# A first transform stage with 128-row matmuls over a block-diagonal table, and a new order of all operations

## The chip, the cores and the metric

The kernel runs on one core of a Trainium2 chip. A core has TensorE (PE, matmuls into PSUM), VectorE (DVE), ScalarE (ACT), GpSimd (POOL), and SyncE (SP), whose queue issues most of the DMAs here; ACT's queue issues a few. Each engine works through its own instructions in the order in which they stand, and semaphores make one engine wait for another. The metric is the device time of one launch in microseconds (us). Three runs of the kernel before took 208.42, 209.37 and 209.37 us; the median is 209.37 us.

## The reference

Two independent halves read inputs of sequence length 2048 and width 640, and their outputs are laid side by side (2048 x 1280, bf16).

```python
# half A: a diagonal complex state-space layer
Lam_bar = jnp.exp(dt * Lam); B_bar = ((Lam_bar - 1.0) / Lam)[:, None] * Bmat
Bu = jnp.einsum("bld,pd->blp", x + 0j, B_bar)
for t in range(L):
    h = Lam_bar[None, :] * h + Bu[:, t, :]
y = 2.0 * jnp.einsum("blp,dp->bld", hseq, Cmat).real + x * Dskip[None, None, :]
# half B: a four-tap convolution of k, times v, a long convolution with ssm_k by FFT, times q
kv = k_shift * v
y_f = rfft(pad(kv)) * rfft(pad(ssm_k))
y = irfft(y_f)[:, :S, :] + kv * ssm_D
return q * y
```

## The kernel before

One SBUF tensor, `arena`, holds everything; `acc` is the whole of PSUM, eight banks. Names such as `s1h0_4` below are those that the program gives its operations: kind, then half or group.

Half A splits the 2048 steps into 128 blocks of 16. Matmuls at L554 and L575 build the input of every level of a 16-step scan (`up2`, `up1`, `up0`; results leave PSUM by ACT or DVE at L571, L595, L620). Then a scan over the 128 blocks runs in two halves of five groups (`coarse`): for each half a matmul that swaps real and imaginary parts (`cs_v`, L646 and L647), a rotation on DVE, the scan itself (L654), a second swap (`cs_k`) and the rotation back, which ends at L660 (`cs_h`). `down` spreads the block states over the 16 steps again (PE at L677 and L679, added back at L695 or L697), and `project` forms the output: 20 matmuls at L714 for each of the sixteen rows of 128 steps (`C0` to `C15`), an addition at L716 and a store at L720. Its factor x times Dskip is an own instruction at L706 (`xd`), on DVE or POOL, and needs rows of x that L705 loads (`ld_r`).

Half B is a transform of length 4096 in two stages, for two halves of 320 channels, first for the filter (`h`) and then for the signal (`k`). Stage 1 (`s1`, L832) handles eight columns per operation. A column holds four channels on four blocks of 32 partitions. The table `F1` has two channel columns (`me` marks the parity of the partition's block of 32), so one matmul covers two channels, 64 partitions: a column takes 2 (halves of the output) x 2 (pairs of channels) matmuls of a 64x64 tile on 64 moving columns, 32 for one operation. The two channel pairs use different row halves of the array and write different PSUM banks. The result, 128x1024, is copied out by ACT or DVE at L837 (`e1`). Stage 2 is L850 with its copies at L863 (`s2`, `e2`), the product of the two spectra is on DVE and POOL at L874 to L881, the way back is L895 with L900 (`r2`) and L916 with L928 (`r1`), and L940 stores.

The signal of half B comes from a chain through one buffer: k is loaded transposed (L769), multiplied by four taps and summed (L197 or L198, L795), multiplied by v (L796), written to DRAM as rows (L802, `pl`) and read back in another layout (L812, `rl`). The second half of the filter (`ld_h1`, L762, four loads) goes into a buffer that `coarse` uses until `cs_h1`; then one small load (`ld_D`, L750) and one small addition (`addD1`, L764) must be done before the first of the ten operations `s1h1` may start.

What runs where and when is a table of numbers written out by hand or by a planner, `ORDER`: `"123A0"` says that operation 123 is issued next, on engine A (A is ACT, V DVE, G POOL, T PE, S SP), with PSUM bank 0. All engines' queues follow from it. `emit` adds the semaphores that the footprints in memory ask for, and an operation that writes PSUM waits until its banks have been copied out.

Of the kernel before, what the change touches and what calls it, by code (L numbers as in the profile page):

```python
# [182 lines left out]
for _name, _n in (("A", 10 * 16 * 130), ("BT", 6400), ("RR", 5120), ("W", 4096), ("G", 8192), ("XT", 10240), ("AS", 10240),  # L183
                  ("Y", 10240), ("T", 6656), ("KT", 2064), ("VT", 6144), ("H0", 5120), ("KV", 5120), ("YS", 2560), ("I3", 192),
                  ("E", 64), ("JS", 128), ("F1", 128), ("IDF", 192), ("DR", 640), ("SK", 20), ("DM", 160),
                  ("PV", 60), ("SMALL", 1400)):
    LAY.part(_name, _n)
# [31 lines left out]
def setup(c):  # L219
# [34 lines left out]
    me, mk = f(2), f(2)  # L254
# [10 lines left out]
    for b, off in ((0, 6144.0), (1, 8192.0)):  # L265
# [5 lines left out]
    P.add("f1", {V: .32}, lambda e: e.tensor_tensor(  # L271
        out=F1.rearrange("p (k s) -> p k s", s=2), in0=bc(s1.rearrange("p (k o) -> p k o", o=1), [128, 64, 2]),
        in1=bc(me.rearrange("p (o s) -> p o s", o=1), [128, 64, 2]), op=ALU.mult), outs=[F1], ins=[s1, me])
# [62 lines left out]
def params(c):  # L336
# [7 lines left out]
    for k, src in enumerate((lam_re, lam_im, ldt_in)):  # L344
        rows = pr[10 * k:10 * k + 10, :]
        P.add("ld_par", {PSP: .1}, lambda e, rows=rows, src=src: e.dma_start(
# [376 lines left out]
class PartB:  # L723
# [91 lines left out]
    def s1(self, what, hf, u):  # L815
# [11 lines left out]
        def mm(e, B):  # L827
            for i in range(8):
                for b in range(2):
                    for l in range(2):  # L830
                        ps = slice(64 * l, 64 * l + 64)
                        e.matmul(B[64 * b:64 * b + 64, 512 * l + 64 * i:512 * l + 64 * i + 64], lhsT=lh[i][ps], rhs=F[ps, b, :], start=True,  # L832
                                 stop=True, tile_position=(64 * l, 64 * b))
        P.add(f"s1{what}{hf}_{u}", {PPE: .27}, mm, ins=lh + [c.F1], group=g, nmm=32)
# [3 lines left out]
            out=out, in_=B.rearrange("p (l n k s) -> p k s l n", n=8, l=2, s=2)), outs=[out], group=g)  # L838
# [192 lines left out]
def plain_order(P):  # L1031
# [125 lines left out]
```

## Time and profile before

| what | value |
|---|---|
| median of three runs | 209.37 us (208.42 to 209.37) |
| span of the profiled execution, first to last instruction | 205.6 us |
| the median less that span | 3.8 us |
| PE busy | 180.7 us, 88% |
| DVE busy | 166.2 us, 81% |
| ACT busy | 142.5 us, 69% |
| POOL busy | 76.4 us, 37% |
| stage 1, L832: matmuls, busy | 1280, 18.2 us |
| copies of stage 1, L837: on ACT, on DVE | 34 and 6 |

A time of its own is not given for the profiled execution, only its span; what lies around the span is taken as the 3.8 us of the table. A profile line of a group reads: source line, engine, operation, what it writes and reads, how often; then busy us and the mean ns of one; then the idle time of the engine just before it and what ended it. A line of the timeline reads: start in us, length in us, engine, line, operation, shapes, count, and in brackets the idle time before it. Consecutive instructions of one line are merged in one row, and its length reaches to the end of the last, which overlaps the start of the next row.

### The profile page before, as it was taken

The page shows a single profiled execution, that of the slowest core. Times are in us where ns is not written, and L with a number is a line of the kernel's source. Part 1 is how long each engine was busy: PE and PEld are TensorE (multiplying, and loading weights), DVE is VectorE, ACT ScalarE, POOL GpSimd, SP SyncE. Part 2 cuts the span into 40 slices and gives each one's busy share as a digit, 9 for nine tenths or more (in the row PEclk, how much of TensorE's full clock was granted, in tenths as well). Part 3 has the DMA queues.
Part 4 walks back from the last instruction along what each step waited for, and adds up shares of the span by engine and source line. Part 5 has one row for each costly group of instructions (what it writes and reads, how often), then busy time and mean ns, then how long its engine had stood idle before and what let it go on. Part 6 is the DMA issues. An engine that isn't in the chain of part 4 may idle for free.

```text
span 205.6 us, 8247 instructions
## 1 busy us (share of the span) xinstructions
PE 180.7 (88%) x3713; PEld 118.7 (58%) x3713; DVE 166.2 (81%) x228; ACT 142.5 (69%) x164; POOL 76.4 (37%) x63
## 2 busy tenths in 40 slices
PE   2399999999999989768759999999999998999891
PEld 0245444554556647447546757546577776887670
DVE  4929349798949698798697989999999899988821
ACT  2628897887994889999738799996999950550000
POOL 8799900000040727037310180684910507120120
PEclk9999999999999999999965899999999999999998
DMA  4999979989999989659948990140962794166866
GB/s 124 160 195 168 183 163 168 136 187 156 228 222 180 267 135 199 109 100 129 134 141 171 161 101 3 40 129 3 212 80 67 171 218 96 66 160 168 227 165 156
DMA packets 107549, 30.20 MB, mean 147 GB/s; under 512 B 102394, under 2 KB 106874, under 8 KB 107514
## 3 DMA queue, kind: packets, MB, share of 16 engines
q1 hardware_dynamic: 107226, 29.35, 77.4%
q8 instruction: 29, 0.48, 1.1%
q10 hardware_dynamic: 288, 0.33, 0.5%
q14 instruction: 6, 0.05, 0.1%
HBM read 10.99 MB, written 7.86 MB: 92 GB/s over the span
## 4 chain that ended last, share of the span: by engine, by line
PE 46%; ACT 24%; DVE 10%; DMA 10%; issue 5%; POOL 1%; SPq 0%; DVEq 0%; ACTq 0%
PE acc L714 14%; PE acc L554 12%; ACT arena L863 8%; ACT arena L837 7%; DMA arena<-in_B_k_dram 6%; PE acc L850 5%; PE acc L679 3%; PE acc L832 3%; PE acc L895 3%; DVE arena L716 2%; PE acc L575 2%; DVE arena L874 2%; ACT arena L198 2%; DVE arena L877 2%; PE acc L916 2%
## 5 line engine op out<-in xcount | busy, mean ns | idle before, releaser
L554 PE MATMUL acc<-arena 128*64 128x512 bf16 x400 | 50.0, 403 | 3.9 <-issue 3.6
L714 PE MATMUL acc<-arena 128*128 128x320 bf16 x320 | 46.0, 300 | 1.4 <-DVE arena L716 0.8
L554 PEld LDWEIGHTS <-arena 128*64 128x64 bf16 x400 | 23.4, 112 | 26.5 <-issue 6.5
L714 PEld LDWEIGHTS <-arena 128*128 128x128 bf16 x320 | 30.4, 98 | 14.4 <-issue 0.9
L837 ACT CAST arena<-acc 128x1024 bf16<-128x1024 f32 x34 | 32.7, 1033 | 5.8 <-PE acc L832 5.6
L863 ACT CAST arena<-acc 128x960 bf16<-128x960 f32 (+1 forms) x37 | 32.5, 907 | 5.7 <-PE acc L850 4.9
L850 PE MATMUL acc<-arena 128*64 128x160 bf16 x512 | 23.2, 238 | 2.5 <-ACT arena L863 1.3
L832 PE MATMUL acc<-arena 64*64 64x64 bf16 x1280 | 18.2, 205 | 6.9 <-ACT arena L837 3.0
L706 POOL TENSOR_TENSOR arena<-arena 128x640 bf16<-128x640 bf16 x9 | 13.4, 1499 | 28.0 <-DMA arena<-in_A_x_dram 28.0
L850 PEld LDWEIGHTS <-arena 128*64 128x64 bf16 x512 | 18.2, 111 | 8.8 <-ACT arena L863 3.7
L900 ACT CAST arena<-acc 128x1024 bf16<-128x1024 f32 x16 | 15.5, 1021 | 10.8 <-PE acc L895 10.8
L832 PEld LDWEIGHTS <-arena 64*64 64x64 bf16 x1280 | 14.5, 117 | 14.0 <-ACT arena L837 6.2
L795 DVE TENSOR_TENSOR arena<-arena 128x2048 bf16<-128x2048 bf16 x14 | 17.8, 1268 | 5.8 <-ACT arena L198 5.5
L198 ACT ACTIVATE arena<-arena 128x2048 bf16<-128x2048 bf16 (+3 forms) x15 | 18.6, 1243 | 5.4 <-DMA arena<-in_B_k_dram 4.2
L697 DVE TENSOR_TENSOR arena<-acc,arena 128x1024 bf16<-128x1024 f32 (+2 forms) x17 | 19.2, 1148 | 1.4 <-ACT arena L863 0.7
L881 POOL TENSOR_TENSOR arena<-arena 128x1280 bf16<-128x1280 bf16 x3 | 8.5, 2821 | 27.5 <-DVE arena L877 27.5
L716 DVE TENSOR_TENSOR arena<-acc,arena 128x640 bf16<-128x640 f32 x16 | 13.3, 832 | 4.9 <-PE acc L714 4.8
L434 POOL TENSOR_TENSOR arena<-arena 128x1280 bf16<-128x1280 bf16 x1 | 2.3, 2331 | 32.1 <-ACT arena L198 32.1
L679 PE MATMUL acc<-arena 128*128 128x512 bf16 (+2 forms) x50 | 13.0, 346 | 0.6 <-ACT arena L837 0.5
L197 DVE TENSOR_SCALAR arena<-arena 128x2048 bf16<-128x2048 bf16 (+2 forms) x17 | 11.8, 699 | 1.2 <-DMA arena<-in_B_k_dram 0.9
L928 DVE TENSOR_TENSOR arena<-acc,arena 128x960 bf16<-128x960 f32 (+1 forms) x12 | 11.9, 1040 | 0.7 <-DMA arena<-in_B_q_dram 0.4
L874 DVE TENSOR_TENSOR arena<-arena 128x2560 bf16<-128x2560 bf16 x8 | 11.9, 1486 | 0.1
(139 smaller groups left out, 269.1 us busy)
## 6 DMA issues: line engine op xcount, KB each, us to landing
out_dram<-arena SPq DMA_DIRECT2D x32, 160.0 KB, 3.1
arena<-in_B_ssm_k_dram SPq DMA_DIRECT2D x8, 320.0 KB, 7.1
kv_rows<-arena SPq DMA_DIRECT2D x5, 512.0 KB, 4.2
arena<-kv_rows SPq DMA_DIRECT2D x8, 320.0 KB, 5.6
arena<-in_A_x_dram SPq DMA_DIRECT2D x16, 160.0 KB, 4.2
arena<-in_B_q_dram SPq DMA_DIRECT2D x8, 320.0 KB, 5.7
arena<-in_A_B_im_dram ACTq DMA_DIRECT2D x1, 160.0 KB
arena<-in_A_B_re_dram ACTq DMA_DIRECT2D x1, 160.0 KB, 2.7
```

The lines of the kernel that those rows point to most:

```text
L198: self.SM = {nc.scalar: lambda out, in_, by: nc.scalar.mul(out, in_, by), nc.vector: vm(nc.vector), nc.gpsimd: vm(nc.gpsimd)}
L554: e.matmul(o[64 * r:64 * r + 64], lhsT=self.BT[j][:, r, d, :], rhs=self.XP[:, d, 2 * q:2 * q + 2], start=(d == 0), stop=(d == 4), skip_gro ...
L679: e.matmul(B[:, o:o + 128 * k], lhsT=c.RR[:, n, j, :], rhs=A[:, j, q:q + k, 0:128], start=not by_pe, stop=True, skip_group_check=True)
L697: e.tensor_tensor(out=o, in0=b, in1=o, op=ALU.add)
L714: e.matmul(B[:, 512 * b:512 * b + 320], lhsT=lh[j], rhs=self.CT[:, j, 320 * b:320 * b + 320], start=(j == 0), stop=(j == 9))
L716: P.add(f"ev_C{i}", {PDVE: dve(640)}, lambda e, B: e.tensor_tensor(out=ys.rearrange("p (b n) -> p b n", b=2), in0=B.rearrange("p (b n) -> ...
L795: P.add(f"ca{d}_{j}", tt, lambda e: e.tensor_tensor(out=t1, in0=t1, in1=t2, op=ALU.add), outs=[t1], ins=[t1, t2])
L832: e.matmul(B[64 * b:64 * b + 64, 512 * l + 64 * i:512 * l + 64 * i + 64], lhsT=lh[i][ps], rhs=F[ps, b, :], start=True, stop=True, tile_pos ...
L837: P.add(f"e1{what}{hf}_{u}", {PACT: act(1024), PDVE: dve(1024)}, lambda e, B: c.CP[e](out=out, in_=B.rearrange("p (l n k s) -> p k s l n", ...
L850: e.matmul(B[64 * s:64 * s + 64, 512 * b + 160 * i:512 * b + 160 * i + 160], lhsT=c.W[:, k, 64 * b:64 * b + 64], rhs=self.AS[hf][:, k, 160 ...
L863: c.CP[e](out=out, in_=b.rearrange("p r (k j n) -> p r k j n", k=n, j=4) if nj > 1 else b.rearrange("p r (k x) -> p r k x", k=n))
L874: P.add(f"pp{hf}", n1, lambda e: e.tensor_tensor(out=pt, in0=X, in1=Yk, op=ALU.mult), outs=[pt], ins=[X, Yk])
```

## The change

The table `F1` gets four channel columns instead of two (`me4` marks which block of 32 partitions a row is in), so it is block-diagonal over all four channels. A column of stage 1 now takes two matmuls of a 128x64 tile on 128 moving columns instead of four of 64x64 on 64. One operation has 16 matmuls instead of 32, the whole program 3079 instead of 3713. The result has the same size and lies in PSUM with the order (column, frequency, channel) instead of (channel pair, column, frequency, channel), and the copy reads it accordingly. The copies, products, loads and stores stay what they were.

```diff
-                  ("E", 64), ("JS", 128), ("F1", 128), ("IDF", 192), ("DR", 640), ("SK", 20), ("DM", 160),
+                  ("E", 64), ("JS", 128), ("F1", 256), ("IDF", 192), ("DR", 640), ("SK", 20), ("DM", 160),
...
-    me, mk = f(2), f(2)
+    me, mk, me4 = f(2), f(2), f(4)
+    P.add("me4", {V: .12}, lambda e: e.tensor_tensor(out=me4, in0=io4, in1=bc(pe_i, [128, 4]), op=ALU.is_equal),
+          outs=[me4], ins=[io4, pe_i])
...
-        out=F1.rearrange("p (k s) -> p k s", s=2), in0=bc(s1.rearrange("p (k o) -> p k o", o=1), [128, 64, 2]),
-        in1=bc(me.rearrange("p (o s) -> p o s", o=1), [128, 64, 2]), op=ALU.mult), outs=[F1], ins=[s1, me])
+        out=F1.rearrange("p (k s) -> p k s", s=4), in0=bc(s1.rearrange("p (k o) -> p k o", o=1), [128, 64, 4]),
+        in1=bc(me4.rearrange("p (o s) -> p o s", o=1), [128, 64, 4]), op=ALU.mult), outs=[F1], ins=[s1, me4])
...
-        P.add("ld_par", {PSP: .1}, lambda e, rows=rows, src=src: e.dma_start(
+        P.add("ld_par", {PSP: .1, PACT: .1}, lambda e, rows=rows, src=src: e.dma_start(
...
-                    for l in range(2):
-                        ps = slice(64 * l, 64 * l + 64)
-                        e.matmul(B[64 * b:64 * b + 64, 512 * l + 64 * i:512 * l + 64 * i + 64], lhsT=lh[i][ps], rhs=F[ps, b, :], start=True,
-                                 stop=True, tile_position=(64 * l, 64 * b))
-        P.add(f"s1{what}{hf}_{u}", {PPE: .27}, mm, ins=lh + [c.F1], group=g, nmm=32)
+                    e.matmul(B[64 * b:64 * b + 64, 128 * i:128 * i + 128], lhsT=lh[i], rhs=F[:, b, :], start=True, stop=True,
+                             tile_position=(0, 64 * b))
+        P.add(f"s1{what}{hf}_{u}", {PPE: .45}, mm, ins=lh + [c.F1], group=g, nmm=16)
...
-            out=out, in_=B.rearrange("p (l n k s) -> p k s l n", n=8, l=2, s=2)), outs=[out], group=g)
+            out=out, in_=B.rearrange("p (n k l s) -> p k s l n", n=8, l=2, s=2)), outs=[out], group=g)
...
-    "48V0 33G0 50S0 123A0 51S0 115G0 122A0 108G0 42G0 49S0 6G0 72G0 7V0 73G0 137S0 1G0 18G0 0G0 30G0 2V0 119G0 8V0 114S0 12V0 465G0 "
...
+    "109G0 31G0 124A0 86V0 49V0 51A0 0G0 6G0 7V0 9V0 459V0 83V0 8V0 12V0 27V0 120V0 25V0 26V0 11V0 1G0 2V0 10V0 43G0 19G0 21V0 28V0 "
...
```

The whole of `ORDER` is replaced, with other engines for some operations: both `addD` go from DVE to POOL, the three parameter loads (`ld_par`) from SP's queue to ACT's. Source lines below L252 move by two in the changed kernel up to stage 1 (L832 stays L832, L764 becomes L766). Three places follow, of before and of the changed kernel.

SP's queue at the start, before: three parameter loads and one half of the first input pair (`ld_x7`, the first row with in_A_x) stand ahead, the other half (`ld_x6`) behind the taps and a part of B.

```order
L346 DMA arena<-in_A_Lambda_im_dram 10x2x64
L346 DMA arena<-in_A_log_dt_dram 10x2x64
L346 DMA arena<-in_A_Lambda_re_dram 10x2x64
L522 DMA_TRANSPOSE arena<-in_A_x_dram 128x5x256
L745 DMA arena<-in_B_shift_k_dram 128x5x4
L489 DMA_TRANSPOSE arena<-in_A_B_im_dram 128x5x256
L522 DMA_TRANSPOSE arena<-in_A_x_dram 128x5x256
L489 DMA_TRANSPOSE arena<-in_A_B_re_dram 128x5x256
```

The same queue in the changed kernel:

```order
L747 DMA arena<-in_B_shift_k_dram 128x5x4
L524 DMA_TRANSPOSE arena<-in_A_x_dram 128x5x256 x2
L491 DMA_TRANSPOSE arena<-in_A_B_re_dram 128x5x256
L491 DMA_TRANSPOSE arena<-in_A_B_im_dram 128x5x256
L771 DMA_TRANSPOSE arena<-in_B_k_dram 128x2048
```

Both halves of the first input pair now follow the first small load, and the parameters are gone from this queue.

PE around the last swap of the coarse scan (`cs_k1`, L646 and L647, in the changed kernel L648 and L649), before; the L832 rows ahead of it are the first three operations of `s1k0`:

```order
L832 LDWEIGHTS arena
L832 MATMUL acc<-arena 64x64
L646 LDWEIGHTS arena
L646 MATMUL acc<-arena 128x512
L647 LDWEIGHTS arena
L647 MATMUL acc<-arena 128x128
L832 LDWEIGHTS arena
```

The same place in the changed kernel; the L679 and L681 rows ahead of it are the first step down (`dn3_0`):

```order
L679 LDWEIGHTS arena
L679 MATMUL acc<-arena 128x128
L681 LDWEIGHTS arena
L681 MATMUL acc<-arena 128x128
L648 LDWEIGHTS arena
L648 MATMUL acc<-arena 128x512
L649 LDWEIGHTS arena
L649 MATMUL acc<-arena 128x128
L832 LDWEIGHTS arena
L832 MATMUL acc<-arena 64x128
```

The swap moved ahead of all ten operations `s1k0`, and a stage 1 matmul now has 128 moving columns.

DVE from the end of the coarse scan (L660) to the first output row (L716), before, with the small addition `addD1` (L764) just ahead of L716:

```order
L649 TENSOR_TENSOR arena<-acc,arena 128x640
L657 TENSOR_TENSOR arena<-arena 128x640
L197 TENSOR_SCALAR arena<-arena 128x2048
L660 TENSOR_TENSOR arena<-arena 128x5x128
...
L874 TENSOR_TENSOR arena<-arena 128x2560
L877 TENSOR_TENSOR arena<-arena 128x8x160
L764 TENSOR_TENSOR arena<-arena 128x80
L716 TENSOR_TENSOR arena<-acc,arena 128x640
```

DVE in the changed kernel (L662 is the end of the scan, L708 the factor of output row 0, L718 the addition of that row):

```order
L651 TENSOR_TENSOR arena<-acc,arena 128x640
L662 TENSOR_TENSOR arena<-arena 128x5x128
L797 TENSOR_TENSOR arena<-arena 128x2048
L197 TENSOR_SCALAR arena<-arena 128x2048
...
L874 TENSOR_TENSOR arena<-arena 128x2560
L877 TENSOR_TENSOR arena<-arena 128x8x160
L708 TENSOR_TENSOR arena<-arena 128x640
L718 TENSOR_TENSOR arena<-acc,arena 128x640
```

And POOL in the changed kernel, where `addD1` now stands (the second L766) behind a convolution sum (L797) and a table product (L329):

```order
L797 TENSOR_TENSOR arena<-arena 128x2048
L329 TENSOR_TENSOR arena<-arena 128x1024
L766 TENSOR_TENSOR arena<-arena 128x80
L329 TENSOR_TENSOR arena<-arena 128x1024
L879 TENSOR_TENSOR arena<-arena 128x8x4x40
```

On DVE a tap multiplication (L197) left its place between the last rotation and the end of the scan, and `addD1` left DVE. On SP's queue the four loads of `ld_h1` are followed by one row of x (`ld_r0`) and then by `ld_D` in the changed kernel; before, both rows of x stood ahead of `ld_h1`, and `ld_D` directly behind it.

More of the change, by code (lines that the diff above doesn't have):

```diff
@@ L270, in setup @@
     P.add("f1_s", {A: .27}, lambda e: e.activation(out=s1, in_=q1, func=FN.Sin, bias=npi, scale=SC13), outs=[s1], ins=[q1, npi])
-    P.add("f1", {V: .32}, lambda e: e.tensor_tensor(
-        out=F1.rearrange("p (k s) -> p k s", s=2), in0=bc(s1.rearrange("p (k o) -> p k o", o=1), [128, 64, 2]),
-        in1=bc(me.rearrange("p (o s) -> p o s", o=1), [128, 64, 2]), op=ALU.mult), outs=[F1], ins=[s1, me])
+    P.add("f1", {V: .42}, lambda e: e.tensor_tensor(
+        out=F1.rearrange("p (k s) -> p k s", s=4), in0=bc(s1.rearrange("p (k o) -> p k o", o=1), [128, 64, 4]),
+        in1=bc(me4.rearrange("p (o s) -> p o s", o=1), [128, 64, 4]), op=ALU.mult), outs=[F1], ins=[s1, me4])
     Wt = c.W = v("W").rearrange("p (k c) -> p k c", c=128)
```

70 rows, old and new, of the table ORDER are left out of this document.

## The prediction

> **What bounds the kernel now.** I read the busy times first, then the chain that ended last, then PE's timeline where the chain leaves PE, and at last sums over stretches.
>
> ```profile
> PE 180.7 (88%) x3713; PEld 118.7 (58%) x3713; DVE 166.2 (81%) x228; ACT 142.5 (69%) x164; POOL 76.4 (37%) x63
> ```
>
> Three engines are near the span, so no engine alone sets it; PE comes nearest. The timeline of PE and DVE and of SP's queue show the one large hole in the second half:
>
> ```profile
> 89.27 0.49 DVE L660 TENSOR_TENSOR arena<-arena 128x640 bf16<-128x640 bf16 x1
> ...
> 89.91 8.05 SPq L762 DMA_DIRECT2D arena<-in_B_ssm_k_dram  x4
> 98.07 1.23 SPq L750 DMA_DIRECT2D arena<-in_B_ssm_D_dram  x1
> ...
> 102.44 1.60 DVE L764 TENSOR_TENSOR arena<-arena 128x80 bf16<-128x80 bf16 x1 [1.51 <-DMA arena<-in_B_ssm_D_dram]
> ...
> 104.13 0.44 PE L832 MATMUL acc<-arena 64*64 64x64 bf16 x32 [2.37 <-DVE arena L764]
> ```
>
> The coarse scan ends at 89.76 (89.27 + 0.49) and frees the buffer of the second filter half. Four loads and a small one are issued until 99.30, have landed at 102.44, DVE adds, and PE starts the second stage 1 (`s1h1`) at 104.13, after 2.37 us without work. Sums over stretches show what follows (us, then PE, PEld, DVE, ACT, POOL busy, then the granted clock):
>
> ```profile
> 101.76:104.13 2.37, 0.00 (x0) 0.03 (x1) 1.70 (x2) 0.72 (x1) 1.90 (x1) 1.00 1.14 309
> 104.66:114.60 9.94, 8.59 (x311) 6.44 (x311) 8.76 (x10) 7.46 (x9) 0.00 (x0) 0.50 0.55 120
> ...
> 104.13:150.80 46.67, 43.84 (x1050) 29.32 (x1050) 43.50 (x45) 39.19 (x43) 21.56 (x10) 0.89 0.56 101
> 150.80:200.20 49.40, 47.94 (x1041) 36.44 (x1040) 42.06 (x50) 21.89 (x24) 12.11 (x6) 1.00 0.61 140
> ```
>
> Half a microsecond after the hole the granted clock is 0.50, for 9.94 us with 8.59 us of PE work, which at full clock would be 4.3 us. From 104.13 to 200.20 PE is busy 43.84 + 47.94 = 91.8 of 96.07 us: the second half is PE's, with 4.3 us of idle time. DVE is close in the first stretch (43.50 of 46.67), so a faster PE gains little there beyond 3 us.
>
> **The change, part by part.**
>
> Stage 1 matmuls. The rows of the old form and the nearest rows of the new one (a 128x64 tile with 128 moving columns is what L575 does):
>
> ```profile
> 51.03 0.71 PE L832 MATMUL acc<-arena 64*64 64x64 bf16 x64
> 51.73 2.45 PE L554 MATMUL acc<-arena 128*64 128x512 bf16 x20
> ...
> 64.00 0.45 PE L832 MATMUL acc<-arena 64*64 64x64 bf16 x32
> 64.38 2.45 PE L554 MATMUL acc<-arena 128*64 128x512 bf16 x20
> ...
> 59.13 1.01 PE L575 MATMUL acc<-arena 128*64 128x128 bf16 x24
> 59.98 2.43 PE L554 MATMUL acc<-arena 128*64 128x512 bf16 x20
> ...
> 69.61 0.64 PE L575 MATMUL acc<-arena 128*64 128x128 bf16 x16
> 70.19 0.60 PE L544 MATMUL acc<-arena 64*64 64x320 bf16 x12
> ```
>
> From start to next start, one old operation takes 0.38 (64.00 to 64.38) and two take 0.70 (51.03 to 51.73); 16 matmuls of the new form take 0.58 (69.61 to 70.19). So half as many matmuls cost 0.20 more: the two row halves no longer run beside each other. All 40 operations: +8.0. Two operations in a row cost 0.06 less than twice one, so a change of tile shape costs some 0.08 (0.06 to 0.10). The new shape is that of L554 and L850, and counting neighbours in the two orders, shape changes on PE fall from 92 to 69: -1.8. After the start of `s1h1` stand 20 operations and 6 fewer changes: +4.0 - 0.5 = +3.5, all where PE sets the pace. The other 20 stand where PE waits for copies or loads, and I count them at nothing; if that cover is gone they cost up to 4.0 - 1.3 = 2.7. Bounds for one operation: +0.10 (no change of shape on either side) and, by the 24 matmuls from 59.13 to 59.98 (35 ns each, 0.57, plus a change), +0.27; for the late 20, +1.5 to +4.9.
>
> By the Trainium skill, "TensorEngine Tiling (Array Packing)", section "When to Use Tiling", a contraction of 64 rows is a case for two row tiles, which is given up here: twice the columns on half the tiles would cost twice the old time, 0.76 and not 0.58, for the late 20 another 3.6. The trace's 0.58 speaks against the full factor.
>
> Copies of stage 1 read PSUM in another order:
>
> ```profile
> L837 ACT CAST arena<-acc 128x1024 bf16<-128x1024 f32 x34 | 32.7, 1033 | 5.8 <-PE acc L832 5.6
> L900 ACT CAST arena<-acc 128x1024 bf16<-128x1024 f32 x16 | 15.5, 1021 | 10.8 <-PE acc L895 10.8
> ```
>
> L900 already reads with the step of 128 words that L837 gets, crosses a bank after four words as L837 will, and takes 1021 against 1033 ns. Cost: 0. The table operation `f1` doubles to 256 elements, and `me4` is new: 2.0 us at most on DVE, at a time when PE works through the inputs; 0.
>
> The start. SP's queue issues one load after the other:
>
> ```profile
> 0.94 0.41 SPq L346 DMA_DIRECT2D arena<-in_A_Lambda_im_dram  x1
> ...
> 2.12 1.57 SPq L522 DMA_TRANSPOSE arena<-in_A_x_dram  x1
> 3.74 0.58 SPq L745 DMA_DIRECT2D arena<-in_B_shift_k_dram  x1
> ...
> 5.74 1.80 SPq L522 DMA_TRANSPOSE arena<-in_A_x_dram  x1
> ...
> DMA to landing us min/median/max: 2.9/4.8/6.6
> ...
> 10.67 7.19 PE acc L554 x40
> ```
>
> PE begins `up2` at 10.67, 4.9 us after the second half of its input was issued, about the median landing time of in_A_x (4.8). In the new order that pair follows the taps alone: 0.94 + 0.58 + 1.80 = 3.3, landing at 8.1, so PE begins some 2.5 us earlier. The parameter loads pass to ACT's queue ahead of the second raw B load; PE needs them for one small matmul only, and ACT is idle there. Behind this, copies and later loads take some of it back. I let 2.2 us arrive at the coarse scan; ends 0 (the k loads set the pace) and 2.5.
>
> The coarse scan. Rows of DVE ahead of the scan's end:
>
> ```profile
> 76.99 0.75 DVE L197 TENSOR_SCALAR arena<-arena 128x2048 bf16<-128x2048 bf16 x1
> 78.17 1.16 DVE L863 CAST arena<-acc 128x960 bf16<-128x960 f32 x1 [0.42 <-ACT arena L620]
> ...
> 87.47 0.82 DVE L649 TENSOR_TENSOR arena<-acc,arena 128x640 bf16<-128x640 f32 x1 [1.08 <-PE acc L647]
> ...
> 88.61 0.75 DVE L197 TENSOR_SCALAR arena<-arena 128x2048 bf16<-128x2048 bf16 x1
> ```
>
> DVE waits 1.08 for the last swap, which stands on PE behind three `s1k0`; now it stands ahead of all ten. The tap at 88.61 (0.75) goes behind the scan's end. One copy of the size at 78.17 (1.16) leaves this part of DVE and one tap (0.75) joins: -0.4. With the 2.2 the scan ends 2.2 + 1.08 + 0.75 + 0.4 = 4.4 earlier, at 85.3. Behind it SP issues four loads (8.05), one row of x and the small load; from the small load's issue to the addition were 102.44 - 98.07 = 4.4:
>
> ```profile
> L705 SPq DMA_DIRECT2D arena<-in_A_x_dram x16: 327/358/3501, 82.8 to 195.4; - x16
> L388 POOL TENSOR_TENSOR arena<-arena 128x80 int32<-128x80 int32 x1 | 0.3, 321 | 0.1
> ```
>
> 85.3 + 8.05 + 0.36 + 4.4 = 98.1. The addition moves to POOL, which is done with what stands ahead by then; its price there lies between 0.32 (80 elements, the row above) and DVE's 1.60. It is nearer to the POOL row: 98.4, 99.7 at most. The second condition is a free bank behind ACT's copies:
>
> ```profile
> 86.60 7.43 ACT L837 CAST arena<-acc 128x1024 bf16<-128x1024 f32 x8
> 93.84 0.80 ACT L695 CAST arena<-acc 128x640 bf16<-128x640 f32 x1
> 94.64 5.77 ACT L863 CAST arena<-acc 128x640 bf16<-128x640 f32 x7
> 101.52 0.96 ACT L863 CAST arena<-acc 128x960 bf16<-128x960 f32 x1 [1.11 <-PE acc L850]
> ```
>
> ACT is through with the filter's copies 2.2 earlier, at 84.4; then 0.80 for the step down that it now copies, 7 copies of 0.93, 0.80, 7 copies in 5.77 and the wait of 1.11: 99.4. So `s1h1` starts at 99.5 instead of 104.13, with the two conditions a microsecond apart: PE has about 0.5 us without work instead of 2.37, and the clock stays at 1.00.
>
> By the Trainium skill, "TensorE: Matmul & The Clock Gate", section "Why this matters for your kernels", idle gaps of PE should stay under some 3 us. The trace's 2.37 was already enough here, so I take 2.37 as the point from which the clock falls.
>
> Late moves of single operations between DVE, ACT and POOL leave each engine below PE's sum; POOL gets two more products of 2.6 us and keeps idle time. 0.
>
> Sum, against the profiled execution: 99.5 + (91.8 - 4.3 + 3.5) + 4.3 idle as before + 5.4 (from 200.20 to the end) = 200.2 us of span, against 205.6. The median lies 3.8 above that span: 204.0.
>
> **The rivals.**
>
> Slower: the hole comes back. One row of x now stands ahead of `ld_D`, and its issue took up to 3.5 us; then the addition ends 3.1 later, PE idles over 2.4 and the clock halves again. Price: 3.1 + 4.3, and ten `s1h1` with 0.20 more at half clock, 2.0: 213.4. It decides from 2.4 us of idle PE. For it: the loads' landing varies. Against it: the bank alone asks for 99.4, so the loads have to be late by over 2.
>
> Smaller gain: the k loads, one buffer for five, set the pace, and the 2.5 of the start is lost: 204.0 + 2.2 = 206.2. For it: each k load has to wait for the taps of the one before it, and that order has not changed.
>
> The page's doubling of stage 1 gives, with the row's 0.38 doubled, 204.0 + 3.6 = 207.6. Against it stands 0.58.
>
> Copies slowed by the new order in PSUM: 24 copies on ACT where ACT sets the pace, at 0.2 each: 4.8, 208.8. Against it: L900.
>
> A new hole elsewhere late: 2.4 + 4.3 = 6.7 more, 210.7.
>
> **How the numbers follow.** A measurement can tell 0.5% from no change, that is 208.3 to 210.4 as the same. Forecast (201 to 206) 0.52; smaller gain 0.10; doubling 0.06; copies and mixtures near no change 0.07; the hole again 0.17; another late hole 0.08. Faster 0.68, same 0.07, slower 0.25. The range reaches from 201 (both bounds of stage 1 and start in its favour) to 211, which holds all but the hole and the lowest tail; for the forecast alone it is 201 to 206.
>
> **What would show it.** `up2` starts near 8 us; L832 shows 640 matmuls and about 0.5 us an operation, its copies still 1.03; the scan's last rotation ends near 85; `s1h1` starts near 99.5 with under 1.5 us of idle PE ahead of it and no stretch with a clock of 0.50; from there to the last output row about 96 us. I am wrong if a clock of 0.50 appears in the second half, if the scan ends after 88, or if the stage 1 copies wait for PE.

## The result and the profile after

The changed kernel took 213.05 to 217.9 us in four runs, median 214.89, against 209.37 before: 1.029 times the time before, with an interval of 1.023 to 1.035. It is 2.9% slower; 204.0 was predicted. The profiled execution on record (217.9, span 216.1) is a disturbed one, so sums over stretches are read from a repeated run of the same kernel (`after_again`, below, span 210.0), and the ratios in this document compare undisturbed runs alone, which is why they need not be the ratio of the medians. The lengths of the single instructions discussed below agree in both profiles.

The page of the changed kernel, busy times and chain of waits, and the chain's line of the page before behind it:

```profile
PE 187.2 (87%) x3079; PEld 126.7 (59%) x3079; DVE 178.7 (83%) x227; ACT 136.9 (63%) x164; POOL 82.5 (38%) x63
...
PE 51%; DVE 27%; DMA 7%; issue 5%; SPq 4%; ACT 3%; POOL 1%; ACTq 1%; DVEq 0%; POOLq 0%
```

```profile
PE 46%; ACT 24%; DVE 10%; DMA 10%; issue 5%; POOL 1%; SPq 0%; DVEq 0%; ACTq 0%
```

DVE has one instruction less than before and is busy 12.5 us longer (10.2 in the repeated run, 176.4); its share of the chain went from 10% to 27%. Its groups, in the repeated run of the changed kernel and then before, show which instructions grew:

```profile
L874 DVE TENSOR_TENSOR arena<-arena 128x2560 bf16<-128x2560 bf16 x8 | 14.3, 1786 | 0.0
L708 DVE TENSOR_TENSOR arena<-arena 128x640 bf16<-128x640 bf16 x8 | 10.4, 1297 | 0.3 <-DMA arena<-in_A_x_dram 0.3
```

```profile
L874 DVE TENSOR_TENSOR arena<-arena 128x2560 bf16<-128x2560 bf16 x8 | 11.9, 1486 | 0.1
L706 DVE TENSOR_TENSOR arena<-arena 128x640 bf16<-128x640 bf16 x7 | 3.3, 487 | 1.7 <-DMA arena<-in_A_x_dram 1.7
```

The same product (L874) and the same x times Dskip (L706, now L708), with the same shapes, take 1786 instead of 1486 and 1297 instead of 487 ns.

**Up to the second stage 1 the times came nearly as predicted**, though not by all of the predicted steps (see the part on why). The timeline of the repeated run: PE and `up2`, the last rotation of the scan, the small loads, the addition, and `s1h1`.

```profile
9.42 3.19 PE L556 MATMUL acc<-arena 128*64 128x512 bf16 x14
...
84.47 0.50 DVE L662 TENSOR_TENSOR arena<-arena 128x640 bf16<-128x640 bf16 x1
...
92.92 2.53 SPq L707 DMA_DIRECT2D arena<-in_A_x_dram  x1
95.55 0.57 SPq L752 DMA_DIRECT2D arena<-in_B_ssm_D_dram  x1
...
97.77 1.16 POOL L766 TENSOR_TENSOR arena<-arena 128x80 bf16<-128x80 bf16 x1 [4.89 <-ACT arena L863]
...
99.79 0.64 PE L832 MATMUL acc<-arena 128*64 128x128 bf16 x16 [0.41 <-issue]
101.93 2.15 PE L832 MATMUL acc<-arena 128*64 128x128 bf16 x64 [1.50 <-DVE arena L718]
```

The scan ends at 84.97, `s1h1` starts at 99.79 after 0.41 us without work (104.13 after 2.37 before). But right behind its first operation stands a new gap of 1.50, released by DVE's L718, the output addition `ev_C0`.

**Then the gain is given back.** The sums over the two stretches from `s1h1` to the start of the last output addition, cut at C5 as in the prediction (us, then PE, PEld, DVE, ACT, POOL busy, then the clock):

```profile
99.79:153.00 53.21, 44.45 (x730) 31.27 (x731) 50.90 (x44) 40.41 (x46) 30.45 (x13) 0.97 0.45 85
153.00:206.40 53.40, 49.75 (x1042) 37.61 (x1038) 43.95 (x47) 24.06 (x26) 14.60 (x7) 0.97 0.62 136
```

The first takes 53.21 instead of 46.67 and DVE is busy in 50.90 of it: the stretch is now DVE's, no longer PE's. The second takes 53.40 instead of 49.40. So 4.3 are gained up to `s1h1`, 6.5 and 4.0 lost after it, 1.8 gained at the end (210.0 - 206.4 = 3.6 instead of 5.4): 4.4 more, which is 210.0 - 205.6. (In the kernel before the last output addition starts at 200.44 and not at the 200.20 of the prediction's cut, so 0.2 of the 4.0 and of the 1.8 belong to the cut.)

Two short stretches inside them ran at half clock:

```profile
118.30:121.72 3.42, 2.94 (x37) 2.45 (x38) 2.69 (x3) 1.00 (x2) 0.72 (x1) 0.50 0.30 96
176.33:179.74 3.41, 3.33 (x133) 2.81 (x134) 2.75 (x3) 0.00 (x0) 1.44 (x1) 0.50 0.31 91
```

That splits the 106.6 us from 99.79 to 206.40. PE is busy in 44.45 + 49.75 = 94.2, of which the half clock makes (2.94 + 3.33) / 2 = 3.1; without it PE's work is 91.1, and the prediction's sum had 91.8 - 4.3 + 3.5 = 91.0. PE has no work in 12.4, where the prediction had 4.3. So PE's work was forecast rightly, the new stage 1 included; what came on top is 8.1 us more of idle PE and 3.1 us of half clock.

Where: DVE, POOL and PE from 109 to 120 in the repeated run.

```profile
111.06 3.90 DVE L874 TENSOR_TENSOR arena<-arena 128x2560 bf16<-128x2560 bf16 x1
114.89 2.88 DVE L708 TENSOR_TENSOR arena<-arena 128x640 bf16<-128x640 bf16 x1
117.90 0.83 DVE L718 TENSOR_TENSOR arena<-acc,arena 128x640 bf16<-128x640 f32 x1
...
110.55 6.87 POOL L881 TENSOR_TENSOR arena<-arena 128x1280 bf16<-128x1280 bf16 x2 [7.14 <-DVE arena L877]
...
118.78 1.54 PE L850 MATMUL acc<-arena 128*64 128x160 bf16 x20 [4.88 <-DVE arena L718]
```

POOL runs two products `pz0`, 6.87 us together, where two that nothing delays take 5.2 (2.60 for one of the kernel before, at 117.60). Beside them DVE's `pp0` takes 3.90 (1.49 elsewhere) and `xd1` 2.88 (0.48 elsewhere): POOL and DVE take turns, each waiting for the other's instruction to end. `ev_C1` is behind both, C1's banks stay occupied, and PE has no work for 4.88 us. The same happens at four other places; the DVE row of each, in time order (`xd0` beside `g_q`, `pq1` beside `pq1`, a tap of `g_k` beside `py1`, `xd9` beside `pz1`), and the last two POOL instructions they meet:

```profile
98.77 2.18 DVE L708 TENSOR_TENSOR arena<-arena 128x640 bf16<-128x640 bf16 x1 [0.26 <-DMA arena<-in_A_x_dram]
...
141.60 3.23 DVE L877 TENSOR_TENSOR arena<-arena 128x1280 bf16<-128x1280 bf16 x1
...
158.20 2.85 DVE L197 TENSOR_SCALAR arena<-arena 128x1024 bf16<-128x1024 bf16 x1
...
172.40 2.90 DVE L708 TENSOR_TENSOR arena<-arena 128x640 bf16<-128x640 bf16 x1
...
157.63 3.13 POOL L879 TENSOR_TENSOR arena<-arena 128x1280 bf16<-128x1280 bf16 x1 [5.53 <-DVE arena L877]
...
171.76 6.01 POOL L881 TENSOR_TENSOR arena<-arena 128x1280 bf16<-128x1280 bf16 x2 [11.00 <-issue]
```

With the usual lengths (0.48 for `xd` and the tap, 0.82 for `pq`, 1.49 for `pp`) the six DVE instructions last 13.7 us too long. DVE instructions that read PSUM are not touched: beside two products on POOL the additions L699 keep their 1.2 us.

```profile
129.47 5.17 POOL L877 TENSOR_TENSOR arena<-arena 128x1280 bf16<-128x1280 bf16 x2 [10.45 <-DVE arena L874]
...
130.74 3.49 DVE L699 TENSOR_TENSOR arena<-acc,arena 128x1024 bf16<-128x1024 f32 x3 [0.70 <-ACT arena L837]
```

That is where the kernel before has put six of its seven products behind `s1h1`. What PE waits for, in the repeated run, lists the price:

```profile
PE acc L850 <- DVE arena L718: 4.9, 1, 4.9
PE acc L916 <- DVE arena L718: 2.2, 1, 2.2
PE acc L681 <- DVE arena L718: 1.7, 1, 1.7
PE acc L832 <- DVE arena L718: 1.5, 1, 1.5
PE acc L895 <- DVE arena L699: 1.2, 1, 1.2
```

Five gaps, 11.5 us, each behind one of these DVE instructions. Of this list the kernel before has only 0.8 behind its output addition, and the 2.4 ahead of `s1h1`.

The theory to be tested (called the waiting theory below): a DVE instruction that takes both inputs from SBUF (or a tap from SBUF to SBUF) cannot run beside a POOL instruction that reads SBUF; the new order of the second half puts such pairs side by side. Rivals: stage 1's new matmuls are the cause; or DVE has simply got too much work.

### The profile page after: what moved, and what is told of

Read it like the earlier page. It is cut to its first block, busy times and chain, and to the rows that moved or that the text cites. A ratio compares the mean times of both kernels' runs of the same rounds, so it can differ in the third digit from the quotient of the medians.

```text
span 216.1 us, 6975 instructions
## 1 busy us (share of the span) xinstructions
PE 187.2 (87%) x3079; PEld 126.7 (59%) x3079; DVE 178.7 (83%) x227; ACT 136.9 (63%) x164; POOL 82.5 (38%) x63
## 4 chain that ended last, share of the span: by engine, by line
PE 51%; DVE 27%; DMA 7%; issue 5%; SPq 4%; ACT 3%; POOL 1%; ACTq 1%; DVEq 0%; POOLq 0%
PE acc L556 15%; PE acc L716 13%; PE acc L832 6%; DVE arena L874 4%; DVE arena L708 4%; PE acc L850 4%; SPq L764 4%; PE acc L577 3%; PE acc L681 3%; DMA arena<-in_B_k_dram 3%; DVE arena L718 3%; DVE arena L877 3%; PE acc L916 3%; DMA arena<-in_A_x_dram 3%; PE acc L895 2%
## 5 line engine op out<-in xcount | busy, mean ns | idle before, releaser
L556 PE MATMUL acc<-arena 128*64 128x512 bf16 x400 | 48.0, 392 | 2.5 <-ACT arena L573 1.4
L716 PE MATMUL acc<-arena 128*128 128x320 bf16 x320 | 48.0, 309 | 0.0
L716 PEld LDWEIGHTS <-arena 128*128 128x128 bf16 x320 | 31.1, 100 | 13.9
L556 PEld LDWEIGHTS <-arena 128*64 128x64 bf16 x400 | 22.1, 109 | 25.4 <-issue 2.4
L850 PEld LDWEIGHTS <-arena 128*64 128x64 bf16 x512 | 19.4, 117 | 12.8 <-DVE arena L718 5.5
L832 PE MATMUL acc<-arena 128*64 128x128 bf16 x640 | 23.8, 230 | 3.5 <-DVE arena L718 1.5
L832 PEld LDWEIGHTS <-arena 128*64 128x64 bf16 x640 | 20.8, 117 | 8.0 <-ACT arena L837 3.1
L881 POOL TENSOR_TENSOR arena<-arena 128x1280 bf16<-128x1280 bf16 x5 | 15.9, 3183 | 19.7 <-issue 11.0
L797 DVE TENSOR_TENSOR arena<-arena 128x2048 bf16<-128x2048 bf16 x14 | 19.4, 1383 | 3.3 <-ACT arena L198 3.0
L708 POOL TENSOR_TENSOR arena<-arena 128x640 bf16<-128x640 bf16 x8 | 12.0, 1511 | 25.8 <-DVE arena L718 19.0
L699 DVE TENSOR_TENSOR arena<-acc,arena 128x1024 bf16<-128x1024 f32 x15 | 17.8, 1215 | 2.6 <-PE acc L681 1.8
L718 DVE TENSOR_TENSOR arena<-acc,arena 128x640 bf16<-128x640 f32 x16 | 13.1, 821 | 8.1 <-PE acc L716 7.5
L197 DVE TENSOR_SCALAR arena<-arena 128x2048 bf16<-128x2048 bf16 (+2 forms) x19 | 15.0, 797 | 3.6 <-POOL arena L388 3.0
L198 ACT ACTIVATE arena<-arena 128x1024 bf16<-128x1024 bf16 (+3 forms) x14 | 16.4, 1198 | 1.6 <-DVE arena L797 0.9
L681 PE MATMUL acc<-arena 128*128 128x512 bf16 (+2 forms) x50 | 12.9, 348 | 1.9 <-DVE arena L718 1.7
L874 DVE TENSOR_TENSOR arena<-arena 128x2560 bf16<-128x2560 bf16 x8 | 14.3, 1786 | 0.0
L895 PE MATMUL acc<-arena 64*128 64x128 bf16 x320 | 12.2, 226 | 1.3 <-DVE arena L699 1.2
```

The source lines that it names most:

```text
L556: e.matmul(o[64 * r:64 * r + 64], lhsT=self.BT[j][:, r, d, :], rhs=self.XP[:, d, 2 * q:2 * q + 2], start=(d == 0), stop=(d == 4), skip_gro ...
L681: e.matmul(B[:, o:o + 128 * k], lhsT=c.RR[:, n, j, :], rhs=A[:, j, q:q + k, 0:128], start=not by_pe, stop=True, skip_group_check=True)
L699: e.tensor_tensor(out=o, in0=b, in1=o, op=ALU.add)
L708: P.add(f"xd{i}", {PDVE: dve(640, .52), PPOOL: 1.5}, lambda e: e.tensor_tensor(out=ys, in0=ys, in1=c.DR, op=ALU.mult), outs=[ys], ins=[ys, ...
L716: e.matmul(B[:, 512 * b:512 * b + 320], lhsT=lh[j], rhs=self.CT[:, j, 320 * b:320 * b + 320], start=(j == 0), stop=(j == 9))
L718: P.add(f"ev_C{i}", {PDVE: dve(640)}, lambda e, B: e.tensor_tensor(out=ys.rearrange("p (b n) -> p b n", b=2), in0=B.rearrange("p (b n) -> ...
```

## Experiments: stage 1 or the order

Stage 1 alone, in the order of before:

```diff
 # the kernel before, its ORDER kept (numbers from 16 on one higher)
+ F1 of 256, me4, 16 matmuls per operation, copy in the new layout: as in the diff above
- "... 17V0 ..."
+ "... 17V0 16V0 ..."     # me, me4
```

> The kernel before with its own order, and only stage 1 in the new form (128 rows, `F1` of four columns, `me4` put behind `me`). Waiting theory (the loss of the changed kernel comes from DVE instructions that have to wait for a running POOL instruction): the order's collisions are absent, so only the price of the new matmuls shows: 20 late operations at 0.07 to 0.20 each, +1.4 to +4.0, 210.5 to 213.5. Rival, stage 1 is the cause: the whole loss of 5.5 shows here, about 215.

Measured: median 207.86 beside 208.08 of the kernel before on the same chip, ratio 1.011 (0.996 to 1.026): no loss that can be told, not the 215 of the rival, and less than the 210.5 to 213.5 that I had expected. The trace shows where the price of the new matmuls went in the profiled execution. From `s1h1` to the last output addition, and the part of it at half clock, then the half clock of the kernel before:

```profile
105.40:202.32 96.92, 93.09 (x1768) 67.58 (x1770) 85.74 (x95) 61.12 (x66) 33.66 (x16) 0.98 0.59 122
105.94:109.35 3.41, 3.32 (x53) 2.61 (x49) 2.98 (x5) 1.92 (x2) 0.00 (x0) 0.50 0.20 79
```

```profile
104.70:114.94 10.24, 8.93 (x313) 6.63 (x314) 9.06 (x9) 7.76 (x9) 0.00 (x0) 0.50 0.54 117
```

At full clock PE works 93.1 - 1.7 = 91.4 us there, 3.9 more than the 91.8 - 4.3 = 87.5 of the kernel before. But behind the hole ahead of `s1h1`, which both have, the half clock lasts 3.4 us here and 10.2 in the kernel before, which loses 1.7 here and 4.5 there. The dearer matmuls are there; in these two executions the clock gives most of their price back.

The order alone, with the old stage 1:

```diff
 # the changed kernel's ORDER (numbers above 16 one lower, me in the place of me4)
- "... 16V0 ..."     # me4
+ "... 16V0 ..."     # me
+ 32 matmuls per operation, F1 of 128, copy as before
```

> The changed kernel's order with stage 1 in the old form (64 rows, 32 matmuls per operation; `me` takes the place of `me4` in the order). Waiting theory: the collisions of DVE with POOL stay, so the time stays near the changed kernel, 211 to 215, and DVE's L708 and L874 still show instructions of 2.8 to 3.9 us. Rival, stage 1 is the cause: about 204, since the earlier start of `s1h1` is kept and the dearer matmuls are gone.

Measured: 217.96 beside 208.08, ratio 1.056 (1.039 to 1.073), above what was expected even of the waiting theory; L874 on DVE has a mean of 1809 ns. The loss is in the order, and with the old stage 1 it is not smaller. That it is larger goes with two things in its trace: `s1h1` starts at 103.86 and not at 99.79, and the clock is 0.50 for 17.2 us of the span in place of 6.8.

## Experiments: taking the collisions away

Two products moved:

```diff
-436G0 ... 425G0
+436V0 ... 425V0     # the two pz0 at 112.95 and 116.09
```

> The changed kernel with only two products `pz0`, those of POOL at 112.95 and 116.09, issued on DVE at the same places in the order (0.82 each). Waiting theory: DVE's `pp0` of 113.45 falls from 3.90 to 1.49 and `xd1` from 2.88 to 0.48, against 1.64 more: `ev_C1` 3.2 earlier, PE's idle time ahead of `s2h1_9` falls from 5.19 to about 2, and the time to 210 to 212 of 214.9. Rival, DVE simply has too much work (nothing depends on what POOL runs at the time): 1.6 more on DVE in its fullest stretch, about 216.5.

Measured: 210.85, ratio 1.025 (1.008 to 1.042) to the kernel before. DVE around C1:

```profile
113.68 1.49 DVE L874 TENSOR_TENSOR arena<-arena 128x2560 bf16<-128x2560 bf16 x1
115.09 0.48 DVE L708 TENSOR_TENSOR arena<-arena 128x640 bf16<-128x640 bf16 x1
```

Both lengths are back, and PE's gap behind this addition is 0.94 instead of 4.88. DVE got two more instructions and the time fell into the range expected of the waiting theory. But the changed kernel did not run beside it on this chip, and its 1.029 (1.023 to 1.035) lies inside this interval: here the lengths are the proof, not the time.

Seven products moved, and `xd0` to POOL:

```diff
-436G0 425G0 599G0 458G0 611G0 634G0 612G0 ... 680V0 682V2 462G0 118S0 392G0
+436V0 425V0 599V0 458V0 611V0 634V0 612V0 ... 462G0 118S0 392G0 680G0 682V2
```

> The changed kernel with seven products of POOL (two `pz0` at 112.95 and 116.09, `pq1` at 144.81, `pz0` at 147.56, `py1` at 162.75, both `pz1` from 176.88) on DVE at the same places in the order, and `xd0` on POOL ahead of `g_q`. Waiting theory: 13.7 us of prolonged DVE instructions go (1.67 + 2.41 + 2.40 + 2.41 + 2.36 + 2.42), 5.7 us of products come to DVE; PE's late holes of 1.5 to 5.2 us close for the greater part, 204 to 209. Rival, DVE simply has too much work: 5 more on DVE, 218 or above.

Measured: 214.64, ratio 1.043 (1.026 to 1.060): neither theory's number. The prolonged instructions are gone but one (`pz0` at 145.59, 1.88), and C4 starts at 142.78 instead of 147.20. Then PE shows a hole that this edit made:

```profile
154.34 1.93 PE L895 MATMUL acc<-arena 64*128 64x128 bf16 x32 [7.33 <-DVE arena L881]
```

The way back (`r20`) needs the last `pz0`, and I had put it on DVE behind everything that stood ahead of it in the table. So one product was put back:

```diff
-... 700G0 ... 458V0
+... 458G0 700G0 ...     # the last pz0 on POOL, ahead of xd4
```

> As the run that moved seven products, but the last `pz0` stays on POOL, ahead of `xd4`, so that the way back (`r20`) no longer waits behind it on DVE. Six products of POOL are on DVE, `xd0` is on POOL ahead of `g_q`. Waiting theory: the hole of 7.3 us of that run goes and nothing else changes, 204 to 208. Rival, too much work on DVE: the same work moves elsewhere, 211 or above.

> The changed kernel once more, unchanged, on the same chip as the three below. Both theories: 213 to 217, and the prolonged DVE instructions (`pp0` 3.9, `xd1` 2.9, `pq1` 3.2, `g_k` 2.8, `xd9` 2.9) stand at the same places, since they follow from the order.

Both on one chip, before at 209.18: the changed kernel 213.51, with the same prolonged instructions at the same places (the rows above), ratio 1.017 (1.005 to 1.030); with most of the collisions gone 208.04, at the upper edge of what was expected, ratio 0.994 (0.988 to 1.000). DVE still has six products more and one smaller one less, so "too much work on DVE" falls. Moving six products from POOL to the busier DVE and one small product the other way made the kernel 5.5 us faster, somewhat more than the 4.3 that it had lost against the kernel before. It does not yet have the whole gain of the first half: `s1h1` still finds PE idle for 1.27 behind C0, and three collisions are left (`pp0` 2.69 beside `xd3`, `xd2` 1.68 and `pp1` 1.65 beside `pz0` and `xd4`).

## Experiments: the disputed wait by itself

One more instruction on POOL in the kernel before, at a place where POOL is idle and DVE multiplies; once one that reads SBUF, once one that only writes.

```diff
+P.add("extra", {PPOOL: 2.6}, lambda e: e.tensor_tensor(out=xt, in0=X[:, :, hi], in1=X[:, :, hi], op=ALU.mult), outs=[xt], ins=[X[:, :, hi]])
```

> The kernel before with one more instruction on POOL, a product of 128x1280 that nobody uses, which can start when the second `pq0` ends (112.66) and so runs beside DVE's `py0` and `pp0`. Waiting theory: it waits for `py0`, then `pp0` waits for it and lasts about 3.9 instead of 1.49; `ev_C1` comes 1.5 to 2.4 later, and the time is 1.3 to 4 above that of before. Rival (POOL and DVE work independently, DVE was only full): no DVE instruction there changes by more than 0.2, time as before.

```diff
+P.add("extra", {PPOOL: 2.6}, lambda e: e.memset(xt, 0.0), outs=[xt], ins=[X[:, :, hi]])     # 128x4096
```

> The kernel before with one more instruction on POOL at the same place as in the run with the added product, but one that only writes (it sets 128x4096 to zero, about 2 us, which nobody uses). If DVE waits only for a POOL instruction that reads SBUF: `py0` and `pp0` keep 0.82 and 1.49, time as before. If it waits for any POOL instruction: `pp0` at about 3.3, time 1 to 3 above before.

DVE's `py0` and `pp0` and POOL's added instruction, first with the product (L883, L874, L881), then with the zeros (L882, L874, L881):

```profile
114.15 0.83 DVE L883 TENSOR_TENSOR arena<-arena 128x1280 bf16<-128x1280 bf16 x1
115.01 3.49 DVE L874 TENSOR_TENSOR arena<-arena 128x2560 bf16<-128x2560 bf16 x1
...
114.26 2.89 POOL L881 TENSOR_TENSOR arena<-arena 128x1280 bf16<-128x1280 bf16 x1 [7.17 <-DVE arena L877]
```

```profile
113.65 0.82 DVE L882 TENSOR_TENSOR arena<-arena 128x1280 bf16<-128x1280 bf16 x1
114.51 1.49 DVE L874 TENSOR_TENSOR arena<-arena 128x2560 bf16<-128x2560 bf16 x1
...
113.67 3.51 POOL L881 MEMSET arena<- 128x4096 bf16 x1 [7.13 <-DVE arena L877]
```

Beside the reading instruction `pp0` ends at 118.50, 1.35 after POOL's end at 117.15, and lasts 3.49. Beside the writing one, which covers `py0` and `pp0` wholly, both keep their length. The mechanism is shown at one place with one edit. The Trainium skill, "SBUF — State Buffer", section "Who interferes with whom", states this rule: a DVE instruction with two SBUF inputs contends with a GpSimd instruction that reads SBUF, not with one that only writes, and the one that starts second waits for the whole of the first; a DVE instruction with at most one SBUF input does not contend, unless it runs in a mode that uses both port pairs, which the section lists as possible for `tensor_scalar`. The two traces agree, 3.49 against 1.49, and so do the additions from PSUM above (1.2). The tap at 158.20, a `TENSOR_SCALAR` that reads one tensor from SBUF (times a factor per partition), took 2.85 instead of 0.48, so it did contend; in which mode it ran no run here shows.

The price in time was overrated: 210.14 beside 209.18, ratio 1.003 (0.998 to 1.007), with the zeros 1.002 (0.997 to 1.006). From the start of the `pq0` ahead of `py0` to `ev_C1` it takes 7.46 us with the product, 5.97 with the zeros and 5.94 in the kernel before, 1.5 more as expected, but of that most is gone at the end. One collision of 2 us cost little in this kernel; that slack behind it took up the rest is argued, not shown. The changed kernel has six.

## Experiments: the two halves of the order

Because nearly the same operations stand ahead of `s1h1` in both orders (one more in the new one, six in the old), the orders can be cut there and joined crosswise.

```diff
 # new_then_old: the new ORDER up to 503T6 (s1h1_9), then what is left in the order of before
 # old_then_new: the order of before up to the same operation, then what is left in the new ORDER
```

> Stage 1 in the new form throughout; the new order up to the first operation of `s1h1`, and from there the order (engines and banks, too) of the kernel before, with one `py0` put ahead of `xd1` on POOL. Waiting theory (the second half of the new order is what costs, by its collisions): `s1h1` starts near 100 as in the changed kernel, and from there to the end it takes what the kernel before took, so 203 to 207. Rival (the early start of `s1h1` is given back by something that both orders share): as before or slower, 209 to 213.

> Stage 1 in the new form throughout; the order of the kernel before up to the first operation of `s1h1`, and from there the new order. Waiting theory: `s1h1` starts near 105 and the collisions follow, 216 to 221. Rival: as before, 207 to 211.

On one chip, before at 208.46: new then old 206.76, ratio 0.991 (0.985 to 0.998); old then new 212.21, ratio 1.023 (1.014 to 1.032). The sign is settled: the first half of the new order is a gain, the second a loss. The loss is smaller than I expected of this run (212.21 lies in neither range); with `xd0` and `xd1` early on POOL, as before has them, two collisions of the six are absent (a smaller one, 1.96 instead of 0.82 on a `pz0`, is new). The gain is smaller than 4.3 too, and the profile of the joined kernel shows why:

```profile
102.24 2.92 DVE L708 TENSOR_TENSOR arena<-arena 128x640 bf16<-128x640 bf16 x1 [2.10 <-DMA arena<-in_A_x_dram]
...
106.15 1.06 PE L832 MATMUL acc<-arena 128*64 128x128 bf16 x16 [3.02 <-DVE arena L248]
```

The row of x for `xd0` is loaded late, `xd0` meets `py0` on POOL, and PE idles for 3.02 behind C0, with a clock of 0.51 in the 5.9 us after it. So the third join loads rows 0 and 1 earlier:

```diff
+679S0 684S0 ahead of the four ld_h1     # ld_r0, ld_r1
+680G0 685G0 right after 410G0           # xd0, xd1 behind ca4_1
+462G0 after 424G0                       # g_q behind py0
```

> As the run with the new order up to `s1h1` and the old one from there, and besides rows 0 and 1 of x are loaded ahead of the second filter half, `xd0` and `xd1` run on POOL right after `ca4_1`, where DVE copies from PSUM, and the third `g_q` goes behind `py0`. Waiting theory: `ev_C0` comes 1.5 to 2 earlier, PE's idle time behind C0 goes, the clock stays at 1.00, 200 to 205. Rival: the end is set by what comes later, no difference from the run without it.

Measured: 205.66, ratio 0.991 (0.987 to 0.996), a little above the range. In the profiled execution the clock is 1.00 throughout, `ev_C0` starts at 98.52 instead of 105.27. It is no better by ratio than the join without it, in whose profile the hole showed.

The last three runs, on one chip, before at 208.98:

```diff
 # r0_old_s1: the same order, stage 1 in the old form
 # r0_gq:     -462G0 after 424G0   +462G0 after 457G0
```

> The order of the run with rows 0 and 1 loaded early (new up to `s1h1`, old behind it), with stage 1 in the old form of 64 rows and 32 matmuls (`me` takes the place of `me4`). If the new form costs what the prediction counted late (0.20 for each of 20 operations less six changes of shape, 3.5 us), this is 3.5 faster: 200 to 203. If its price lies beside DVE's work, as the run with stage 1 alone suggests, the time is the same within 1 us.

> The run with rows 0 and 1 loaded early, with the third `g_q` (an int32 product on POOL, 1.89 us, beside which `cx4` took 2.66 instead of 1.22) moved behind the `py0` that runs beside DVE's additions from PSUM. Waiting theory: `cx4` is back at 1.22, `e1h1_0` and everything on DVE up to `ev_C1` 1.4 earlier; in the time 0 to 1.5 us less. Rival: no change in the length of `cx4`.

> The run with rows 0 and 1 loaded early once more, unchanged, on the same chip as the two others: 0.987 to 0.996 of the kernel before.

The repeated kernel 205.01, ratio 0.987 (0.981 to 0.993). With `g_q` moved 204.22, ratio 0.983 (0.977 to 0.989); the intervals overlap, so a gain of this last move is not shown in the time, only in the length of `cx4`. The row of `cx4`, before and after that move:

```profile
104.87 2.57 DVE L798 TENSOR_TENSOR arena<-arena 128x2048 bf16<-128x2048 bf16 x1
```

```profile
103.75 1.22 DVE L798 TENSOR_TENSOR arena<-arena 128x2048 bf16<-128x2048 bf16 x1
```

and the stretch from `s1h1` to C5 in that kernel:

```profile
101.15:146.21 45.06, 43.20 (x729) 29.90 (x729) 42.27 (x43) 39.19 (x44) 25.73 (x12) 1.00 0.54 99
```

45.06 us, where the changed kernel needs 53.21. This version is 1.7% faster than the kernel before and beats both.

The old stage 1 in the same order: 207.97, ratio 0.999 (0.993 to 1.004). The prediction's price would have made it 3.5 faster than the new one (205.01), and I had by then expected no difference; it is no faster, and by the medians some 3 us slower. Its twelve runs spread from 204.56 to 212.99, the four of the new one from 204.64 to 205.62. From `s1h1` to the last output addition, with the new form, then with the old one and the part of it at half clock:

```profile
102.28:198.18 95.90, 91.40 (x1769) 66.46 (x1770) 85.62 (x93) 62.35 (x68) 37.70 (x18) 1.00 0.58 120
```

```profile
102.70:197.45 94.75, 89.93 (x2089) 64.36 (x2090) 85.08 (x92) 61.96 (x68) 37.02 (x18) 0.98 0.59 121
109.11:112.52 3.41, 3.41 (x107) 2.45 (x106) 3.31 (x4) 2.73 (x4) 0.00 (x0) 0.50 1.10 199
```

PE's work at full clock is 91.4 us with the new form and 89.9 - 1.7 = 88.2 with the old one. So the new form does cost PE 3.2 us late, near the 3.5 of the prediction. That the runs with it are not slower must have another reason. A candidate is the clock: over the span it is 0.960 to 0.990 in the twelve runs of the old form and 0.994 to 1.000 in the four of the new. Where it first falls in the old form:

```profile
88.00:92.00 4.00, 1.64 (x128) 1.30 (x128) 2.49 (x4) 2.75 (x4) 3.86 (x1) 1.00 1.02 152
92.00:96.00 4.00, 3.75 (x78) 3.20 (x80) 1.89 (x2) 3.14 (x5) 2.90 (x3) 0.57 1.06 148
```

PE waits for the copies of `s1k0` and has one gap of 1.41 inside an operation, for which the profile shows no cause (the run of the order alone has one of 1.23 at the same place); it works 1.64 of 4 us, and the clock then falls to 0.57. With the new form it works 3.30 us in the same window and the clock stays at 1.00. But the execution shown here is the fastest of the old form, 204.56, against 205.06 for the profiled one of the new: it lost nothing to the other. That the clock is the reason of the 3 us is therefore argued, not shown.

## Why the prediction was wrong

- **The step that failed** is this one: "Late moves of single operations between DVE, ACT and POOL leave each engine below PE's sum; POOL gets two more products of 2.6 us and keeps idle time. 0." It added up each engine's work and did not ask what runs beside what. The moves (net three more products on POOL, eleven instead of eight) made six DVE instructions wait for POOL, 13.7 us in all; DVE's busy time to C5 rose from 43.50 to 50.90 and took over that stretch. With it fell the term "4.3 idle as before": PE has no work in 12.4 us, 11.5 of them in the five gaps behind these instructions, and 3.1 us of half clock came on top. With six products taken off POOL the same order takes 0.994 instead of 1.017 of the time before. The trace of before held the sign of it: `addD1` took 1.60 beside a product on POOL (`addD0`, the same addition, 0.53 with POOL idle), and the prediction used that 1.60 as a plain length of DVE.
- The rival "a new hole elsewhere late" (0.08) is what happened, five times and not once; its 210.7 has one hole of 2.4. The chance was too small because no place was named for it. The price of another rival, the hole that comes back (213.4), lies near the measured time by chance: its hole ahead of `s1h1` did not come. A sign of being wrong that the prediction named, a clock of 0.50 in the second half, did appear.
- "`s1h1` starts at 99.5 ... about 0.5 us without work": right in the numbers, 99.79 (100.74 in the profile on record) and 0.41, but in part by luck. The row of x ahead of the small load took 2.53 to issue, not 0.36, and from the small load's issue to the addition were 2.2, not 4.4. "stays at 1.00" held there but not later: in the hole of 4.88 us the clock falls to 0.50.
- The start: `up2` begins at 9.42, not 8.1, so 1.25 of the 2.5 came; PE reaches it straight from another group of matmuls (L516, from 7.58 on) and hardly waits for its inputs (0.4 in all). The scan's end, 84.97 against 85.3, was right as a whole all the same, so steps in between gained more than the sum gave them; which ones, no run here separates.
- Stage 1: "+4.0 - 0.5 = +3.5" late was right as work of PE (91.4 against 88.2 us at full clock in the best order, 91.1 against the sum's 91.0 in the changed kernel). A single operation ahead of a step down takes 0.57 instead of 0.38 from start to next start, as priced; ahead of an `up` matmul, whose tile has the same shape, two take 0.89 instead of 0.64. What the prediction missed is that this work need not show in the time: alone it changes nothing that can be told, and in the best order the kernel with the old form is no faster. The rival in which stage 1's time doubles (207.6) falls: 0.57 is not 0.76.
- "Copies of stage 1 ... Cost: 0": right, 1031 against 1033 ns on ACT; the rival of slowed copies falls.

The row behind the last point, in the repeated run:

```profile
L837 ACT CAST arena<-acc 128x1024 bf16<-128x1024 f32 x33 | 31.8, 1031 | 6.3 <-PE acc L832 6.2
```

What stays open: why the clock is lower with the old form of stage 1, which bears on why the new order with the old form is as slow as 1.056, and what else sets the time there. How much of the loss is waiting and how much is the half clock the sums above tell for one execution, not for the average of the runs.

## What to carry to other kernels

Where an instruction of one engine can hold up one of another, as POOL and DVE do here, sums of busy time do not price a move between them: a product on POOL (2.6 us) beside DVE work from SBUF costs DVE up to 2.4 us of waiting here, some three times the 0.82 us that the product itself takes on DVE. Put POOL's reading work beside DVE instructions that take their input from PSUM, and check each placed pair in the timeline: an instruction that lasts longer than its group's usual length is the sign. When a new order wins in one half and loses in the other, cut both orders at a point where the same work is done and join them crosswise.

## What was unexpected of the hardware

- DVE and POOL wait for each other in turn: with DVE products from SBUF on one side and two POOL products on the other, the POOL pair took 6.87 instead of 5.2 us, and DVE's instructions 3.90 and 2.88 instead of 1.49 and 0.48.
- PE's clock fell without a long gap: after 4 us in which PE worked 1.64 us, with a longest gap of 1.41, the clock was 0.57 in the next 4 us, while 1.50 without work behind C0 in the changed kernel left it at 1.00. In the traces of this case the half clock comes in stretches of 3.41, 6.83 or 10.24 us. The prediction's single point of 2.37 us of idle time is therefore no rule here. The Trainium skill, "TensorE: Matmul & The Clock Gate", section "What's actually happening", lets the clock fall after an idle window of some 3.4 us; these 4 us were thinly used, not idle.
